# Attention on one core: three weighted bit patterns instead of four in the rows that VectorE exponentiates

## Chip, core and metric

One core of a Trainium2 chip runs the whole program. The metric is the device time of one execution in microseconds. The engines are named as the profile names them: PE (TensorE, matmuls; PEld its weight loads), ACT (ScalarE), DVE (VectorE), POOL (GpSimd, idle after the first microseconds), and SP, which issues most transfers.

## What is computed

```python
B, S, D, H = 1, 2048, 448, 16          # Dh = 28; inputs bf16
qkv = (x @ wqkv).reshape(B, S, 3, H, Dh).transpose(2, 0, 3, 1, 4)
q, k, v = qkv[0], qkv[1], qkv[2]
scores = einsum("bhqd,bhkd->bhqk", q, k) * Dh ** -0.5
p = softmax(scores, axis=-1)
o = einsum("bhqk,bhkd->bhqd", p, v)
return o.transpose(0, 2, 1, 3).reshape(B, S, D) @ wo
```

It is self-attention of 16 heads over 2048 positions with its projections. The kernel takes no maximum out of the scores; at the end it tests the softmax sums, and if they are out of bounds it would run a second, general program (`_general`). On these inputs only the first program (`_fast`) runs.

## The kernel before

**Tiling.** The 16 heads form four groups g of four. A *unit* u is one group and one chunk c of 512 queries: 16 units, u = 4g + c. A unit has 16 key blocks kt of 128 keys. One key block of one unit is a *row*, r = 16u + kt, 256 in all. A row has four *tiles*, one per head: 128 keys by 512 queries of scores, one bank of PSUM.

**Scores (L875).** For each tile PE multiplies KT (28 rows deep, stationary) with QT into a bank. Q is scaled on its way into QT (L512, L514), so that a score is log2 of the wanted exponential, times 1024.

**Exponentials, two ways.** Most rows are *ACT rows*: one activation (L937) takes three banks or two in turn (banks 0 to 2, banks 3 and 4) and writes exponentials in bf16 into PT, a ring of NPT = 47 tile slots; a group of three or two is not split over the end of the ring. 63 rows, listed in `PLAN["rows"]`, are *DVE rows*. For each of their four tiles DVE adds a constant to the score, clamps it at zero and converts it to int16 (L899, tile DY): read as a half float, that bit pattern is a rough exponential. Then it makes, for the whole row at once, copies of the four tiles with 200, 446 and 751 added (L907, tile DS; the numbers are `PHASE`). The errors of the four patterns differ, and their sum is a good exponential. DY and DS have three buffers each. The score banks of DVE rows come from three shared banks ("M"), where the accumulators and the projections live as well.

**Value matmuls (L843, `pv`).** For each row PE multiplies V (stationary, 32 columns a head: 28 of V, a column of ones for the softmax sum, zeros) with the tile's exponentials; four heads run side by side in four column strips, and I call four such matmuls a *pass*. An ACT row takes one pass; a DVE row takes four: one with DY, three with DS, all with the same V, added up in the accumulator. The passes of all rows go in order of the rows.

**Around it.** PE makes xT (L526), the projections to QT and KT (L543) and V (L560), DVE evacuates them (L514, L516), in the first unit as they are needed and later in between. At a unit's end DVE copies the accumulator out (L711), the sums go through DRAM and back (L717 to L725, reciprocal L721), and L727 normalizes into the tile XO; the output projection (L698, L686) follows in the last head group, the last unit has its own tail (L777 to L820). CK and FLAG (L969 to L981) are the test of the sums.

**What sets the order.** Every operation goes to `_Prog.add` with a duration, a priority and what it depends on. `schedule` places all of them on the five engines by these figures, and each engine's instructions are emitted in that order, with semaphores where another engine is waited for. `CFG` and `PLAN` hold the constants: the DVE rows, when late projections are due, how far ahead a DVE row's scores start (`dlead`, in tiles). Where PE would have too little work within a stretch, `fill_to` adds *zero passes* (L472: four matmuls of zeros, added to the open accumulator), and where that can't be done, zero matmuls behind the scores (L878, "padding").

Of the kernel before, what the change touches and what calls it, by code (L numbers as in the profile page):

```python
# [7 lines left out]
ALU = mybir.AluOpType  # L8
AX = mybir.AxisListType
FP32 = mybir.dt.float32  # L10
BF16 = mybir.dt.bfloat16
# [52 lines left out]
class _Prog:  # L64
# [264 lines left out]

LOG2E = 1.4426950408889634  # L330

PHASE = (0, 200, 446, 751)
FONE = 1024.0
ZADD = 15.0 * FONE - FONE * 2.4248887
ZLO = -ZADD


CFG = {"late": 4.5, "load": 1.5, "load0": 18, "dcost": 2.3, "dlead": 31.025180582, "aslack": 232.311784294, "opp": 0.0, "oload": 2.5, "klead": 0.407460656, "vlag": 0.113823454, "hot1": 45000.0, "hotm": 3600.0, "nslack": 2266.270469736, "dlook": 20.0, "plook": 475.482288433, "rcost": 4.9, "rlead": 1.0, "rend": 4, "rgap": 2, "acost": 0.4455, "dprio": -0.035050185, "nride": 2, "rslack": 300.0, "stail": 24, "jprio": -2.321750811, "sdpen": 6.865040263, "rcostx": -0.000676632}

PLAN = {  # L340
    "rows": [9, 14, 19, 20, 25, 33, 36, 39, 43, 48, 51, 52, 54, 61, 62, 69, 75, 79, 80, 85, 87, 95, 96, 98, 103, 108, 110, 115, 117, 120, 131, 133, 134, 140, 142, 144, 148, 149, 154, 160, 170, 172, 176, 177, 178, 180, 184, 191, 194, 197, 201, 207, 211, 212, 215, 218, 223, 225, 229, 231, 239, 240, 241],
    "late": [1.08724689, 1.671681906, 1.586461994, 1.492212309, 1.992884293, 1.888874123, 1.952599148, 2.085365324, 2.327563384, 2.683517599, 2.852937922, 3.53079825, 3.236530611, 3.738744089, 4.578206384, 3.853855012, 4.352187387, 4.127154975, 4.601545874, 4.748366198, 5.016471943, 5.791742663, 6.023704782, 6.452540401, 5.67492232, 6.933850091, 5.567830617, 6.240906859, 8.033147916, 7.787869286, 7.499426139, 7.210279289, 7.346492082, 7.304458952, 7.814524164, 8.966950855, 8.707648667, 8.756221306],
}


def _fast(nc, x, wqkv, wo, out, n_heads=16):
# [9 lines left out]
    NK = NST  # L356
# [2 lines left out]
    NQT = QCH // 128  # L359
    HC = H * 32  # L360
    GD = 4 * DH
    NPT = 47
    NDR = 3
    NDS = 3
    NPH = len(PHASE)
    NMENG = "dve"
# [13 lines left out]
    P = _Prog()  # L380
    es = ExitStack()
    with es:
        def sb(name, shape, dt):
            return es.enter_context(nc.sbuf_tensor(name, shape, dt))
# [7 lines left out]
        QT = sb("QT", [128, G, S], BF16)  # L392
        KT = sb("KT", [128, G, S], BF16)
        V = sb("V", [128, NK, HC], BF16)
        PT = sb("PT", [128, NPT * 512], BF16)
        DY = sb("DY", [128, NDR, 2048], I16)
        DS = sb("DS", [128, NPH - 1, NDS, 2048], I16)
# [12 lines left out]
        ps = es.enter_context(nc.psum_tensor("ps", [128, 8 * 512], FP32))  # L410
# [24 lines left out]
        def load_w(en, t, i0, i1):  # L435
# [11 lines left out]
                      dur=300, prio=-12, name="iota")  # L447
        id_f_op = P.add("dve", lambda e: e.tensor_scalar(id_f[:, :], iota_i[:, :], 0.0, None, ALU.is_equal),
                        deps=[io_op], dur=250, prio=-10, name="id_f")
# [6 lines left out]
        def zero_pass(acc_open, t):  # L456
# [12 lines left out]
            def emit(e):  # L469
                ins = None  # L470
                for h in range(4):
# [13 lines left out]
                       deps=[id_f_op], dur=100, prio=-6, name="sel")  # L485
        grp_wo = _DmaGroup("wo")
        dma_wo = []
        for g in range(G):
            for h in range(4):
# [3 lines left out]
                                    deps=[ms_wop], after=dma_wo[-1:] + [q_last["sp"]], dur=300, prio=-5, name=f"dma_wo{g}{h}", dma_group=grp_wo))  # L493
# [53 lines left out]
            kq_ev[(t, g, c)] = job(f"p{t}_{g}_{c}", prio, mms,  # L547
                                   ((lambda: dst[:, g, c * 512:(c + 1) * 512]), (lambda b: bank(b))), early, evac_eng=eng, mul=QSCALE if t == 0 else None)

        v_ev = {}  # L550

        def proj_v(g, c, prio, early):
            mms = []
# [52 lines left out]
        rows = PLAN["rows"]  # L606
        if rows is None:
# [5 lines left out]
            rows = []  # L613
# [15 lines left out]
        k = 0  # L629
# [194 lines left out]
        def pv(u, kt):  # L824
            g, c = units[u]
            r = u * NK + kt
            if r in n_row:
                ri = n_row[r] % NDR
                rk = n_row[r] % NDS
                terms = [DY[:, ri, :]] + [DS[:, k, rk, :] for k in range(NPH - 1)]  # L830
                parts = [[t_.bitcast(FP16)[:, h * 512:(h + 1) * 512] for h in range(4)] for t_ in terms]
                deps_of = [row_ops[r]] + [[o_] for o_ in row_ev[r]]
                slots = []
            else:
                slots = [tile_slot[(u, kt, h)] for h in range(4)]
                parts = [[PT[:, pi * 512:(pi + 1) * 512] for _, pi in slots]]
                deps_of = [list({id(tile_ev[(u, kt, h)]): tile_ev[(u, kt, h)] for h in range(4)}.values())]

            def f_pv(e, k, p_):
                ins = None  # L840
                b = pv_open[u].banks[0]
                for h in range(4):
                    ins = e.matmul(ps[32 * h:32 * h + 32, b * 512:(b + 1) * 512], V[:, kt, (4 * g + h) * 32:(4 * g + h + 1) * 32],  # L843
                                   p_[h], start=(kt == 0 and k == 0), stop=(kt == NK - 1 and k == len(parts) - 1), tile_position=(0, 32 * h))
                return ins
            base_pr = (u - 60.0 if u == NU - 1 and kt >= NK - 3 else u + (kt + 4) / NK)
            for k, p_ in enumerate(parts):
                first, fin = kt == 0 and k == 0, kt == NK - 1 and k == len(parts) - 1
                op = P.add("pe", (lambda e, k=k, p_=p_: f_pv(e, k, p_)), deps=deps_of[k]
                           + [v_ev[(g, kt // 4)]], acq=(("M", 1) if first else None),  # L850
                           after=[last_pv[0]], kind="c", units=1.0, act=512.0, acc=(True if first else False if fin else None), prio=base_pr, name=f"PV{u}_{kt}" + (f"_{k}" if k else ""))
                last_pv[0] = op
                if first:
                    pv_open[u] = op
                if r in n_row:
                    row_pv[(n_row[r], k)] = op
            for s_ in slots:
                slot_last[s_] = op
            if kt == NK - 1:
                (last_unit if u == NU - 1 else post_unit)(u, op)  # L860
# [7 lines left out]
        n_row = {}  # L868
# [45 lines left out]
        for gi, (kind, idx, b0) in enumerate(items):  # L914
            tl = [tiles[i] for i in idx]
            w = len(tl)
            deps = []
            for (u, kt, h) in tl:
                g, c = units[u]
# [9 lines left out]
            else:  # L929
# [4 lines left out]
                      acq=("M", 1) if b0 is None else None)  # L934
# [3 lines left out]
                       deps=[s] + [slot_last.get(("A", p0 + j)) for j in range(w)], after=[last_exp[0]], dur=66 + w * 426.67, prio=pr, name=f"E{gi}",  # L938
# [10 lines left out]
            if todo_rows and 4 * todo_rows[0] - CFG["dlead"] <= idx[-1] and (nxt < NDS or (nxt - NDS, NPH - 1) in row_pv):  # L949
                r = todo_rows[0]  # L950
# [7 lines left out]
            while pv_next < NT // 4 and all(4 * pv_next + j in done for j in range(4)):  # L958
                u, kt, _ = tiles[4 * pv_next]
# [7 lines left out]
        for lo, hi, rdeps, pr_ in ((0, NE, rs_ops, NU - 0.5), (NE, NE + 16, rs_last, -30.0)):  # L967
# [3 lines left out]
                       deps=[c1], dur=60 + w_, prio=pr_, name=f"CK2_{lo}")  # L971
# [4 lines left out]
        def f_ck(e):  # L976
            b = f_ck.op.banks[0]
            return e.matmul(ps[0:1, b * 512:b * 512 + 1], CKM[:, :], ONE[:, :], start=True, stop=True)
        c4 = P.add("pe", f_ck, deps=[c3, ms_one], dur=100, prio=-34.5, name="CKS", acq=("M", 1))
        f_ck.op = c4  # L980
        P.flag_op = P.add("dve", (lambda e: e.tensor_scalar(FLAG[:, :], ps[0:1, c4.banks[0] * 512:c4.banks[0] * 512 + 1], 127.5, None, ALU.is_ge)),  # L981
                          deps=[c4], dur=80, prio=-34.5, name="FLAG", rel=[(c4, 0)])
# [15 lines left out]
def _general(nc, x, wqkv, wo, out, n_heads=16):  # L998
# [12 lines left out]
    NK = NST  # L1011
# [8 lines left out]
    NPT = 32  # L1020
# [10 lines left out]
    P = _Prog()  # L1031
    es = ExitStack()
    with es:
        def sb(name, shape, dt):
            return es.enter_context(nc.sbuf_tensor("gen_" + name, shape, dt))
# [9 lines left out]
        V = sb("V", [128, NK, HC], BF16)  # L1045
# [14 lines left out]
        ps = es.enter_context(nc.psum_tensor("gen_ps", [128, 8 * 512], FP32))  # L1060
# [10 lines left out]
        for i in range(XG):  # L1071
# [3 lines left out]
                               dur=60, prio=(-10 if i == 0 else -9.7 + 0.01 * i), name=f"dma_x{i}", dma_group=grp, nbytes=(n1 - n0) * 128 * D * 2))  # L1075
        wview = wqkv.rearrange("(it p) c -> p it c", p=IT)
        dma_w = []
        for t in (1, 0, 2):
            grp = _DmaGroup(f"gen_w{t}")
            dma_w.append((t, P.add("sp", (lambda e, t=t: e.dma_start(w_raw[0:IT, :, t * D:(t + 1) * D], wview[:, :, t * D:(t + 1) * D])),  # L1080
                                   dur=60, prio={1: -9.9, 0: -9.8, 2: -9.0}[t], name=f"dma_w{t}", dma_group=grp, nbytes=D * D * 2)))
# [9 lines left out]
        def i32v(ap):  # L1091
# [4 lines left out]
                        deps=[ms_wqk], dur=150, prio=-11, name="ms_wqk1")  # L1096
        ms_wqk2 = P.add("dve", lambda e: e.memset(wqk6[XQ:IT, NIT - 1, 1, :, :, AUGR:AUGR + 3], 0.0),
                        deps=[ms_wqk1], dur=150, prio=-11, name="ms_wqk2")
        io_op = P.add("pool", lambda e: e.iota(iota_i[:, :], [[1, 128]], base=0, channel_multiplier=-1),
                      dur=600, prio=-12, name="iota")  # L1100
# [3 lines left out]
                       deps=[ms_wv], dur=300, prio=-8, name="ms_wv1")  # L1104
        ms_wv2 = P.add("pool", lambda e: e.memset(wv3[XQ:IT, NIT - 1, :, VONE:VONE + 1], 0.0),
                       deps=[ms_wv1], dur=300, prio=-8, name="ms_wv2")
# [5 lines left out]
        for g in range(G):  # L1112
            for h in range(4):
# [3 lines left out]
                                    deps=[ms_wop], after=dma_wo[-1:], dur=60, prio=-5, name=f"dma_wo{g}{h}", dma_group=grp_wo))  # L1117

        id_f_op = P.add("dve", lambda e: e.tensor_scalar(id_f[:, :], iota_i[:, :], 0.0, None, ALU.is_equal),
                        deps=[io_op], dur=250, prio=-10, name="id_f")  # L1120
# [46 lines left out]
        for n0 in range(0, NST, TPB):  # L1167
            for it in range(NIT):
                nn = min(TPB, NST - n0)

                def mk_tr(it=it, n0=n0, nn=nn):
                    def f(e):
                        b = f.op.banks[0]
                        ins = None
                        for j in range(nn):
# [5 lines left out]
                f = mk_tr()  # L1181
                tr = P.add("pe", f, deps=[id_b_op] + xdeps, dur=70 * nn, prio=-10 + 0.001 * n0 + 0.0001 * it, name=f"xT_tr{it}_{n0}",
                           acq=(start_pool(), 1))
                f.op = tr
                en = evac_engine() if n0 < 4 else "act"
                deps = [tr] + ([ms_xT] if it == NIT - 1 else [])
                ev = P.add(en, emit_copy(en, (lambda it=it, n0=n0, nn=nn: xT[0:IT, it, n0 * 128:(n0 + nn) * 128]),
                                         (lambda tr=tr, nn=nn: bank_bf(tr.banks[0])[0:IT, 0:nn * 128])),
                           deps=deps, dur=(nn * 128 + 80) / 1.1, prio=-10 + 0.001 * n0, name=f"xT_ev{it}_{n0}", rel=[(tr, 0)])
# [14 lines left out]

        qt_ev = {}
        kt_ev = {}
        v_ev = {}
        act_only = [False]

        fillers = []  # L1210
# [281 lines left out]
        for j in range(-KOFF, NB + PVLAG + 1):  # L1492
            ja = j + KOFF
            a = a_steps[ja] if 0 <= ja < NA else None
            b = b_steps[j] if 0 <= j < NB else None
            deps = []
# [8 lines left out]
            if b is not None:  # L1505
                ui_b, kt, bp = b
# [9 lines left out]
            if a is not None or b is not None:  # L1516
                qh = []

                def f_qa(e, a=a, b=b, ja=ja, qh=qh):
# [10 lines left out]
                    if b is not None:  # L1530
# [3 lines left out]
                        if a is None:  # L1534
# [3 lines left out]
                           name=f"QA{j}", acq=((("B", 1) if a is not None else ("T", 2)) if b is not None else None))  # L1538
                qh.append(qa)
                last_pe[0] = qa  # L1540
            if a is not None:
# [7 lines left out]
                if (ja % SPU) == 0 and pm_t1[ub] is not None:  # L1549
                    rdeps.append(pm_t1[ub])  # L1550
                red = P.add("dve", (lambda e, o_ap=o_ap, i_ap=i_ap: e.tensor_reduce(o_ap, i_ap, AX.X, ALU.max, negate=True)),
                            deps=rdeps, after=[last_red[0]], dur=1131, prio=float(ui_a), name=f"R{ja}")
# [6 lines left out]
            if b is not None:  # L1559
                ui_b, kt, bp = b  # L1560
                cb, gb = units[ui_b]
                if a is not None:
                    qh2 = []
                    qb = P.add("pe", mk_b(qh2, 2 * bp + 1, gb, kt, cb), deps=[augev_of[ui_b]], after=[last_pe[0]], dur=216, prio=ui_b + 0.5,
                               name=f"QB{j}", acq=("B", 1))
# [5 lines left out]
                for jj, (qop, bi) in enumerate(qops):  # L1571
                    h = 2 * bp + jj
# [20 lines left out]
            while pv_queue and (pv_queue[0][0] <= j or j >= NB):  # L1593
                _, u_, k_, hs_ = pv_queue.pop(0)
# [126 lines left out]
```

## Time and profile before

| | |
|---|---|
| median of three runs | 372.25 us (372.24 to 372.35) |
| the profiled execution | 372.08 us |
| its span | 370.3 us |
| ACT busy | 353.3 us (95%) |
| PE busy | 360.2 us (97%) |
| DVE busy | 336.0 us (91%) |
| POOL busy | 3.4 us |
| transfers | 9.93 MB, 27 GB/s on average |

A busy share is time in which an engine has an instruction under way. PE's matmuls overlap each other and their ends are modelled, so its share says less than the others'; neighbours on ACT and DVE overlap by some hundredths of a microsecond, so an instruction's duration is a little more than its pace. "A <- B" in a row of waits says that A stood until B was done; "issue" is time for which the profile shows no cause. The granted clock is the share of TensorE's clock that the throttle let through.

### The profile page before, as it was taken

To read this page: it belongs to the slowest core of one execution; us is meant where nothing else is said; L and a number is where in the kernel's file an instruction comes from. 1 tells how busy PE (TensorE), PEld (TensorE's weight loads), DVE (VectorE), ACT (ScalarE), POOL (GpSimd) and SP (SyncE) were. 2 spreads that over 40 slices of the span, in tenths; PEclk is the share of its full clock that TensorE was granted. 3 is DMA by queue.
4 is the path that set the end of the run, shared out by engine and by line. 5 is a ranking of instruction groups with operands and counts; after the bars stand their busy time and mean duration, and the time that the engine had idled before them with its cause. 6 is when DMAs were issued, how large, how long until landed. Compare 5 with 4: busy or idle time off the path is not lost.

```text
span 370.3 us, 9208 instructions
## 1 busy us (share of the span) xinstructions
PE 360.2 (97%) x4056; PEld 120.3 (32%) x4056; DVE 336.0 (91%) x581; ACT 353.3 (95%) x314; POOL 3.4 (1%) x9
## 2 busy tenths in 40 slices
PE   8999999999999999999999999999999999999996
PEld 4443233233233233333234322322222222323323
DVE  6578999799999999899999999999999999999613
ACT  2999999999999999999999999999999999999992
POOL 3000000000000000000000000000000000000000
PEclk9999999999999999999999999999999999999999
DMA  8400000000000000000010000000000000100111
GB/s 250 124 2 3 4 29 4 32 2 4 31 2 4 30 18 17 2 12 21 4 32 5 30 3 3 30 4 29 3 31 4 31 2 31 46 10 28 64 40 52
DMA packets 12549, 9.93 MB, mean 27 GB/s; under 512 B 4768, under 2 KB 10656, under 8 KB 12504
## 3 DMA queue, kind: packets, MB, share of 16 engines
q1 hardware_dynamic: 11704, 8.63, 7.7%
q8 instruction: 32, 0.52, 0.6%
q10 hardware_dynamic: 800, 0.66, 0.5%
q14 instruction: 13, 0.11, 0.1%
HBM read 7.23 MB, written 2.06 MB: 25 GB/s over the span
## 4 chain that ended last, share of the span: by engine, by line
ACT 63%; PE 22%; DVE 13%; issue 1%
ACT PT L937 63%; PE ps L875 8%; DVE DY L899 7%; PE ps L843 6%; DVE DS L907 5%; PE ps L543 2%; PE ps L472 2%; PE ps L698 1%; PE ps L560 1%; PE ps L526 1%; DVE OTS L711 0%; PE ps L777 0%; DVE OUTS L686 0%; DVE QT L514 0%; PE ps L746 0%
## 5 line engine op out<-in xcount | busy, mean ns | idle before, releaser
L937 ACT ACTIVATE PT<-ps 128x1536 bf16<-128x1536 f32 (+1 forms) x310 | 350.3, 1379 | 2.9 <-PE ps L875 1.9
L899 DVE TENSOR_SCALAR DY<-ps 128x512 int16<-128x512 f32 x252 | 163.3, 680 | 6.3 <-PE ps L875 5.7
L875 PE MATMUL ps<-QT,KT 28*128 28x512 bf16 x1024 | 162.6, 384 | 4.4 <-ACT PT L937 1.4
L907 DVE TENSOR_SCALAR DS<-DY 128x2048 int16<-128x2048 int16 x189 | 124.8, 679 | 0.3
L875 PEld LDWEIGHTS ps<-QT,KT 28*128 28x128 bf16 x1024 | 42.0, 91 | 132.1 <-ACT PT L937 84.4
L843 PE MATMUL ps<-PT,V 128*32 128x512 bf16 x772 | 66.2, 385 | 0.7 <-DVE DY L899 0.2
L843 PE MATMUL ps<-DS,V 128*32 128x512 f16 x756 | 64.7, 384 | 0.5 <-DVE DS L907 0.2
L543 PE MATMUL ps<-xT,w_raw 112*32 112x512 bf16 x512 | 34.9, 381 | 0.0
L843 PEld LDWEIGHTS ps<-PT,V 128*32 128x32 bf16 x772 | 16.8, 94 | 32.3 <-issue 25.8
L843 PEld LDWEIGHTS ps<-DS,V 128*32 128x32 bf16 x756 | 16.8, 94 | 30.3 <-issue 19.4
L472 PE MATMUL ps<-ZM,ZW 128*32 128x512 bf16 x272 | 25.0, 414 | 1.2 <-DVE ZM L454 1.2
L843 PE MATMUL ps<-DY,V 128*32 128x512 f16 x252 | 24.8, 384 | 0.3 <-DVE QT L514 0.3
L686 DVE CAST OUTS<-ps 128x448 bf16<-128x448 f32 x14 | 8.7, 621 | 9.5 <-PE ps L698 8.6
L560 PE MATMUL ps<-w_raw,xT 112*128 112x112 bf16 x256 | 17.1, 214 | 0.0
L543 PEld LDWEIGHTS ps<-xT,w_raw 112*32 112x32 bf16 x512 | 12.0, 95 | 13.3 <-issue 2.9
L560 PEld LDWEIGHTS ps<-w_raw,xT 112*128 112x128 bf16 x256 | 13.0, 98 | 6.2 <-issue 3.9
L516 DVE CAST KT<-ps 128x512 bf16<-128x512 f32 x16 | 11.0, 685 | 3.6 <-PE ps L543 3.6
L514 DVE TENSOR_SCALAR QT<-ps 128x512 bf16<-128x512 f32 x15 | 10.3, 684 | 1.9 <-PE ps L543 1.9
L698 PE MATMUL ps<-wop,XO 128*128 128x448 bf16 x48 | 11.9, 356 | 0.0
L516 DVE CAST V<-ps 128x448 bf16<-128x448 f32 x16 | 9.9, 616 | 1.3 <-PE ps L560 1.3
L472 PEld LDWEIGHTS ps<-ZM,ZW 128*32 128x32 bf16 x272 | 6.8, 100 | 11.9 <-issue 9.5
L711 DVE COPY OTS<-ps 128x512 f32<-128x512 f32 x15 | 10.2, 679 | 0.0
(50 smaller groups left out, 71.4 us busy)
## 6 DMA issues: line engine op xcount, KB each, us to landing
RB<-scr_r SPq DMA_DIRECT2D x14, 256.0 KB
out_dram<-OUTS SPq DMA_DIRECT2D x14, 112.0 KB, 1.7
XO<-in_x_dram SPq DMA_DIRECT2D x3, 448.0 KB, 7.3
w_raw<-in_wqkv_dram SPq DMA_DIRECT2D x2, 392.0 KB, 6.7
wop<-in_wo_dram SPq DMA_DIRECT2D x16, 24.5 KB
XO<-in_x_dram SPq DMA_DIRECT2D x1, 224.0 KB, 3.5
XO<-in_x_dram ACTq DMA_DIRECT2D x1, 224.0 KB, 3.8
scr_l<-OTS SPq DMA_DIRECT2D x14, 8.0 KB
```

What stands on the lines that cost most here:

```text
L472: ins = e.matmul(ps[32 * h:32 * h + 32, b * 512:(b + 1) * 512], ZW[:, :], ZM[:, :], start=shut, stop=shut, skip_group_check=not shut, tile ...
L514: fe = (lambda e: e.tensor_scalar(evac[0](), evac[1](hold[0].banks[0]), mul, None, ALU.mult))
L516: fe = (lambda e: e.tensor_copy(evac[0](), evac[1](hold[0].banks[0])))
L543: ins = e.matmul(ps[32 * h:32 * h + 32, b * 512:(b + 1) * 512], w_raw[0:IT, it, col:col + 32], xT[0:IT, it, c * 512:(c + 1) * 512], start= ...
L560: ins = e.matmul(ps[:, b * 512 + j * GD:b * 512 + (j + 1) * GD], xT[0:IT, it, n * 128:(n + 1) * 128], w_raw[0:IT, it, 2 * D + g * GD:2 * D ...
L698: return e.matmul(bank(hold[0].banks[0])[:, 0:D], OTN[:, gg, n * 128:(n + 1) * 128], wop[:, gg, :], start=(gg == 0), stop=(gg == G - 1))
L711: accev = P.add("dve", (lambda e: e.tensor_copy(OTS[:, ub, :], bank(pv_open[u].banks[0]))), deps=[last_pv, ots_last[ub]], dur=610, prio=pr ...
L843: ins = e.matmul(ps[32 * h:32 * h + 32, b * 512:(b + 1) * 512], V[:, kt, (4 * g + h) * 32:(4 * g + h + 1) * 32], p_[h], start=(kt == 0 and ...
L875: ins = e.matmul(bank(b), KT[32 * h:32 * h + rows, g, kt * 128:(kt + 1) * 128], QT[32 * h:32 * h + rows, g, c * QCH:(c + 1) * QCH], start= ...
L899: o1 = P.add("dve", (lambda e, ri=ri, h=h, s=s: e.tensor_scalar(DY[:, ri, h * 512:(h + 1) * 512], bank(s.banks[0]), ZLO, ZADD, ALU.max, AL ...
L907: row_ev[r] = [P.add("dve", (lambda e, k=k: e.tensor_scalar(DS[:, k, rk, :], DY[:, ri, :], float(PHASE[k + 1]), None, ALU.add)), deps=row_ ...
L937: ex = P.add("act", (lambda e, p0=p0, w=w, bf=bf: e.activation(PT[:, p0 * 512:(p0 + w) * 512], bank(bf(), w), AF.Exp, scale=ESCALE)), deps ...
```

## The change

A DVE row has three patterns instead of four, with 0, 344 and 682 added, and they are no longer summed alike: their weights are 1, 101/128 and 80/128. The weights are not put on the patterns but on V. A new tile VW holds, for two head groups in turn, two weighted copies of V, which DVE makes from V: for each quarter of the keys (four key blocks, 128x512 elements) of each group in which a DVE row occurs, one scalar multiplication per weight, 32 in all. The first pass of a DVE row reads V as before, the second and third read VW. DS has two parts instead of three, PT has 43 slots instead of 47. There are 67 DVE rows instead of 63, at other places in part, and the constants of the order are new throughout; `vwlead` says how far ahead of its row, in units, a weighted copy is due.

```diff
-PHASE = (0, 200, 446, 751)
+PHASE = (0, 344, 682)
+WTERM = (1.0, 101.0 / 128.0, 80.0 / 128.0)
 FONE = 1024.0
-ZADD = 15.0 * FONE - FONE * 2.4248887
+ZADD = 15.0 * FONE - FONE * 1.6365345
 ZLO = -ZADD
...
-    "rows": [9, 14, 19, 20, 25, 33, 36, 39, 43, 48, 51, 52, 54, 61, 62, 69, 75, 79, 80, 85, 87, 95, 96, 98, 103, 108, 110, 115, 117, 120, 131, 133, 134, 140, 142, 144, 148, 149, 154, 160, 170, 172, 176, 177, 178, 180, 184, 191, 194, 197, 201, 207, 211, 212, 215, 218, 223, 225, 229, 231, 239, 240, 241],
+    "rows": [9, 14, 19, 21, 26, 32, 36, 37, 43, 48, 51, 54, 57, 58, 61, 67, 74, 78, 83, 85, 90, 95, 96, 99, 103, 104, 107, 111, 113, 118, 119, 126, 128, 133, 136, 142, 143, 145, 147, 155, 160, 164, 170, 171, 175, 176, 180, 181, 187, 190, 192, 194, 197, 199, 207, 208, 211, 215, 216, 219, 221, 228, 229, 232, 239, 242, 243],
...
-    NPT = 47
+    NPT = 43
...
+        VW = sb("VW", [128, 2, NPH - 1, NK, 128], BF16)
...
-        v_ev = {}
+        v_ev, vw_ev, vw_used = {}, {}, {}
...
+            if r in n_row and (g, kt // 4) not in vw_ev:
+                c4 = kt // 4
+                vw_ev[(g, c4)] = [P.add("dve", (lambda e, k=k: e.tensor_scalar(VW[:, g % 2, k, 4 * c4:4 * c4 + 4, :], V[:, 4 * c4:4 * c4 + 4, g * 128:(g + 1) * 128],
+                                                                              WTERM[k + 1], None, ALU.mult)),
+                                        deps=[v_ev[(g, c4)], vw_used.get((g % 2, c4))], dur=200, prio=u + kt / NK - CFG["vwlead"], name=f"VW{k}_{g}_{c4}")
+                                  for k in range(NPH - 1)]
+
+            def weights(k, h):
+                return V[:, kt, (4 * g + h) * 32:(4 * g + h + 1) * 32] if k == 0 else VW[:, g % 2, k - 1, kt, 32 * h:32 * h + 32]
...
-                    ins = e.matmul(ps[32 * h:32 * h + 32, b * 512:(b + 1) * 512], V[:, kt, (4 * g + h) * 32:(4 * g + h + 1) * 32],
-                                   p_[h], start=(kt == 0 and k == 0), stop=(kt == NK - 1 and k == len(parts) - 1), tile_position=(0, 32 * h))
+                    ins = e.matmul(ps[32 * h:32 * h + 32, b * 512:(b + 1) * 512], weights(k, h), p_[h], start=(kt == 0 and k == 0), stop=(kt == NK - 1 and k == len(parts) - 1), tile_position=(0, 32 * h))
...
-                           + [v_ev[(g, kt // 4)]], acq=(("M", 1) if first else None),
+                           + [v_ev[(g, kt // 4)] if k == 0 else vw_ev[(g, kt // 4)][k - 1]], acq=(("M", 1) if first else None),
...
+                    if k:
+                        vw_used[(g % 2, kt // 4)] = op
```

In the changed kernel the lines stand a little lower: scores L888, padding L891, exponentials L950, DY L912, DS L920, VW L843, value matmuls L855, zero passes L474.

More of the change, by code (lines that the diff above doesn't have):

```diff
@@ L330 @@
 LOG2E = 1.4426950408889634
-PHASE = (0, 200, 446, 751)
+PHASE = (0, 344, 682)
+WTERM = (1.0, 101.0 / 128.0, 80.0 / 128.0)
 FONE = 1024.0
-ZADD = 15.0 * FONE - FONE * 2.4248887
+ZADD = 15.0 * FONE - FONE * 1.6365345
 ZLO = -ZADD
-CFG = {"late": 4.5, "load": 1.5, "load0": 18, "dcost": 2.3, "dlead": 31.025180582, "aslack": 232.311784294, "opp": 0.0, "oload": 2.5, "klead": 0.407460656, "vlag": 0.113823454, "hot1": 45000.0, "hotm": 3600.0, "nslack": 2266.270469736, "dlook": 20.0, "plook": 475.482288433, "rcost": 4.9, "rlead": 1.0, "rend": 4, "rgap": 2, "acost": 0.4455, "dprio": -0.035050185, "nride": 2, "rslack": 300.0, "stail": 24, "jprio": -2.321750811, "sdpen": 6.865040263, "rcostx": -0.000676632}
+CFG = {"late": 4.5, "load": 1.5, "load0": 18, "dcost": 2.3, "dlead": 31.565328345, "aslack": 232.311784294, "opp": 0.0, "oload": 2.5, "klead": 0.388752986, "vlag": 0.115386484, "hot1": 45000.0, "hotm": 3600.0, "nslack": 2278.659670856, "dlook": 20.0, "plook": 477.119826734, "rcost": 4.9, "rlead": 1.0, "rend": 4, "rgap": 2, "acost": 0.4455, "dprio": 0.137295812, "nride": 2, "rslack": 300.0, "stail": 24, "jprio": -2.367501222, "vwlead": 0.517534586, "sdpen": 6.828329237, "rcostx": -0.000676632}
@@ L340 @@
 PLAN = {
-    "rows": [9, 14, 19, 20, 25, 33, 36, 39, 43, 48, 51, 52, 54, 61, 62, 69, 75, 79, 80, 85, 87, 95, 96, 98, 103, 108, 110, 115, 117, 120, 131, 133, 134, 140, 142, 144, 148, 149, 154, 160, 170, 172, 176, 177, 178, 180, 184, 191, 194, 197, 201, 207, 211, 212, 215, 218, 223, 225, 229, 231, 239, 240, 241],
-    "late": [1.08724689, 1.671681906, 1.586461994, 1.492212309, 1.992884293, 1.888874123, 1.952599148, 2.085365324, 2.327563384, 2.683517599, 2.852937922, 3.53079825, 3.236530611, 3.738744089, 4.578206384, 3.853855012, 4.352187387, 4.127154975, 4.601545874, 4.748366198, 5.016471943, 5.791742663, 6.023704782, 6.452540401, 5.67492232, 6.933850091, 5.567830617, 6.240906859, 8.033147916, 7.787869286, 7.499426139, 7.210279289, 7.346492082, 7.304458952, 7.814524164, 8.966950855, 8.707648667, 8.756221306],
+    "rows": [9, 14, 19, 21, 26, 32, 36, 37, 43, 48, 51, 54, 57, 58, 61, 67, 74, 78, 83, 85, 90, 95, 96, 99, 103, 104, 107, 111, 113, 118, 119, 126, 128, 133, 136, 142, 143, 145, 147, 155, 160, 164, 170, 171, 175, 176, 180, 181, 187, 190, 192, 194, 197, 199, 207, 208, 211, 215, 216, 219, 221, 228, 229, 232, 239, 242, 243],
@@ new lines @@
+    "late": [1.299322759, 1.822557006, 2.163875537, 1.596356936, 2.063296816, 1.856206612, 1.946155059, 2.196917245, 2.351631723, 2.650591028, 2.763613996, 3.528403009, 3.047534614, 3.721148513, 4.223385591, 3.69651624, 3.88002907, 4.051839957, 4.449835317, 4.560752685, 5.643247141, 5.99397256, 6.330386924, 6.513825751, 5.809406098, 6.003720398, 6.187280726, 6.225029866, 8.237463635, 8.012219161, 7.61108487, 7.334748232, 7.574370741, 6.838411391, 7.65064537, 7.734259839, 8.315962664, 7.954788714],
@@ L1206, in _general @@
         kt_ev = {}
-        v_ev = {}
+        v_ev, vw_ev, vw_used = {}, {}, {}
         act_only = [False]
```

## The prediction

> **What bounds the kernel now.** I read the page's busy times first, then the busy time of each engine by stage, then what ACT waited for, and last the chain of waits. The page gives 370.3 us of span and these shares:
>
> ```profile
> PE 360.2 (97%) x4056; PEld 120.3 (32%) x4056; DVE 336.0 (91%) x581; ACT 353.3 (95%) x314; POOL 3.4 (1%) x9
> ```
>
> Three engines are above 90%, so the mean says little. By stage (stage, its length, then busy us of PE, weight loads, DVE, ACT and POOL, then the granted clock):
>
> ```profile
> 10.00:60.00 50.00, 49.10 (x558) 18.01 (x557) 41.68 (x73) 50.00 (x45) 0.00 (x0) 1.00 0.10 26
> 60.00:110.00 50.00, 49.26 (x586) 16.44 (x584) 46.73 (x80) 49.95 (x45) 0.00 (x0) 1.00 0.04 13
> 110.00:160.00 50.00, 49.12 (x576) 17.17 (x576) 48.45 (x83) 49.86 (x45) 0.00 (x0) 1.00 0.05 13
> 160.00:210.00 50.00, 49.74 (x606) 16.54 (x605) 49.14 (x85) 49.57 (x44) 0.00 (x0) 1.00 0.06 19
> 210.00:260.00 50.00, 48.81 (x551) 14.42 (x547) 49.87 (x85) 49.90 (x46) 0.00 (x0) 1.00 0.05 13
> 260.00:310.00 50.00, 48.79 (x532) 13.84 (x531) 49.88 (x87) 50.00 (x46) 0.00 (x0) 1.00 0.04 13
> 310.00:345.00 35.00, 34.55 (x366) 11.39 (x366) 34.93 (x63) 34.12 (x31) 0.00 (x0) 1.00 0.09 30
> ```
>
> ACT has hardly a hole: its largest loss in a 50 us stage is 0.43 us, and 0.88 us from 310 to 345. DVE is as full from 160 to 345 us, but has 8.3 us free from 10 to 60. What ACT waited for (total, times, longest):
>
> ```profile
> ACT QT L512 <- PE ps L543: 5.6, 1, 5.6
> ACT PT L937 <- PE ps L875: 1.9, 3, 0.8
> ACT PT L937 <- PE ps L878: 0.7, 1, 0.7
> ```
>
> The 5.6 us lie before the first exponential; between exponentials ACT waited 1.9 us in three holes. So the span is a head of 10 us, a packed train of exponentials, and a short tail. Pieces of the chain of waits (start, us, what) give the pace of each engine in a row of its own work:
>
> ```profile
> 1.22 3.60 PE ps L472 x32
> 9.99 76.04 ACT PT L937 x67
> 165.12 0.60 DVE DS L907
> 165.72 1.20 DVE DY L899 x2
> 201.63 0.98 PE ps L843 x16
> 310.78 0.76 PE ps L843 x12
> ```
>
> ACT takes 76.04 / 67 = 1.135 us an exponential, 2.27 us for a triple and a pair, 0.454 us a tile. DVE takes 0.60 us for a first step (DY) and 0.60 us for a phase copy (DS), though one lasts 0.68: neighbours overlap. PE takes 0.98 - 0.76 = 0.22 us for four matmuls more.
>
> **The change, ACT.** Four more rows go to DVE, 16 tiles of 772. The order has 151 triples, 151 pairs and one single, where it had 154, 154 and two:
>
> ```profile
> L937 ACT ACTIVATE PT<-ps 128x1536 bf16<-128x1536 f32 x154 | 245.3, 1593 | 2.9 <-PE ps L875 1.9 <-PE ps L878 0.7
> L937 ACT ACTIVATE PT<-ps 128x1024 bf16<-128x1024 f32 x154 | 180.6, 1173 | 0.0
> L937 ACT ACTIVATE PT<-ps 128x512 bf16<-128x512 f32 x2 | 1.2, 718 | 0.0
> ```
>
> That is 3 x 2.27 + 0.6 = 7.4 us off an engine that has no holes, all on the path.
>
> **The change, DVE.** Its groups:
>
> ```profile
> L899 DVE TENSOR_SCALAR DY<-ps 128x512 int16<-128x512 f32 x252 | 163.3, 680 | 6.3 <-PE ps L875 5.7
> L907 DVE TENSOR_SCALAR DS<-DY 128x2048 int16<-128x2048 int16 x189 | 124.8, 679 | 0.3
> L516 DVE COPY xT<-ps 112x512 bf16<-112x512 bf16 x16 | 6.3, 420 | 3.7 <-PE ps L526 3.7
> L969 DVE TENSOR_SCALAR CK<-RS 128x240 f32<-128x240 f32 x1 | 0.3, 275 | 0.0
> ```
>
> 16 first steps more: 16 x 0.60 = +9.6 us. Phase copies 189 to 134: 55 x 0.60 = -33.0 us. New are 32 weighted copies VW of 128x512 bf16, which the trace does not show. From below, a quarter of a phase copy's elements at its pace is 0.15 us; from above, a first step with as many elements is 0.60 us. Below nothing is excluded, as it is added work on a serial engine. I take 0.25 us: the 240-element scalar operation lasts 0.275, the 512-element copy out of PSUM 0.42, and neighbours overlap by 0.08. So +8.0 us (4.8 to 19.2), and DVE falls from 336.0 by 15.4 us (by 4.2 to 18.6). [...]
>
> Where the first copies stand, DVE in the first unit, around the first V cast. Before:
>
> ```order
> L516 COPY xT<-ps 112x512 x4
> L516 CAST V<-ps 128x4x4x28
> L516 CAST KT<-ps 128x512
> L516 COPY xT<-ps 112x512
> L899 TENSOR_SCALAR DY<-ps 128x512
> L516 COPY xT<-ps 112x512 x3
> ```
>
> Now:
>
> ```order
> L518 COPY xT<-ps 112x512 x4
> L518 CAST V<-ps 128x4x4x28
> L843 TENSOR_SCALAR VW<-V 128x512 x2
> L518 CAST KT<-ps 128x512
> L518 COPY xT<-ps 112x512
> L912 TENSOR_SCALAR DY<-ps 128x512
> L518 COPY xT<-ps 112x512 x3
> ```
>
> Two VW have moved in ahead of the KT cast, on which the scores of the third key chunk, and so ACT, wait. The cover is there:
>
> ```profile
> 15.39 0.62 DVE L516 CAST V<-ps 128x448 bf16<-128x448 f32 x1 [1.26 <-PE ps L560]
> 17.00 0.69 DVE L516 CAST KT<-ps 128x512 bf16<-128x512 f32 x1 [0.98 <-PE ps L543]
> ```
>
> DVE stands 0.98 us before that cast; two copies at 0.25 fit, at 0.60 they cost 0.2 us. The other six of this unit lie in the 8.3 us that DVE has free from 10 to 60. Costed at nothing. The new waits: a VW waits for its V cast on the same engine, and for value matmuls two head groups back, long done; a DVE row's second and third passes on PE wait for VW instead of V, with scores for ACT queued behind them. As VW is due half a unit (the constant 0.52) ahead of its row, the row's own phase copy stays the later of the two, and this wait is costed at nothing too.
>
> From 160 us on DVE has no such holes, so the balance counts there. From row 96 to the last DVE row the plan before has 41 DVE rows and 105 ACT rows; the new one 45 and 103. ACT needs 4 x 0.454 = 1.815 us a row: 190.6 and 186.9 us. DVE needs 41 x 7 x 0.60 = 172.2 us, now 45 x 6 x 0.60 = 162.0. For its other work it had 18.4 us, and has 24.9, out of which ten VW take 2.5. So it is looser than before by some 4 us, and by 0.5 us even with VW at 0.60. The pattern in the last DVE rows, DVE before:
>
> ```order
> L899 TENSOR_SCALAR DY<-ps 128x512 x2
> L721 RECIPROCAL RS<-LT 128x16
> L907 TENSOR_SCALAR DS<-DY 128x2048 x2
> L899 TENSOR_SCALAR DY<-ps 128x512 x2
> L907 TENSOR_SCALAR DS<-DY 128x2048
> L899 TENSOR_SCALAR DY<-ps 128x512 x2
> L907 TENSOR_SCALAR DS<-DY 128x2048
> ```
>
> Now:
>
> ```order
> L912 TENSOR_SCALAR DY<-ps 128x512 x4
> L920 TENSOR_SCALAR DS<-DY 128x2048
> L912 TENSOR_SCALAR DY<-ps 128x512 x2
> L920 TENSOR_SCALAR DS<-DY 128x2048
> L912 TENSOR_SCALAR DY<-ps 128x512 x2
> L729 TENSOR_TENSOR XO<-RB,OTS 128x512
> L912 TENSOR_SCALAR DY<-ps 128x512 x2
> ```
>
> Fewer copies stand between first steps, so score banks come free sooner.
>
> **The change, PE.** Its groups:
>
> ```profile
> L843 PE MATMUL ps<-PT,V 128*32 128x512 bf16 x772 | 66.2, 385 | 0.7 <-DVE DY L899 0.2
> L843 PE MATMUL ps<-DS,V 128*32 128x512 f16 x756 | 64.7, 384 | 0.5 <-DVE DS L907 0.2
> L472 PE MATMUL ps<-ZM,ZW 128*32 128x512 bf16 x272 | 25.0, 414 | 1.2 <-DVE ZM L454 1.2
> L843 PE MATMUL ps<-DY,V 128*32 128x512 f16 x252 | 24.8, 384 | 0.3 <-DVE QT L514 0.3
> L878 PE MATMUL ps<-ZM 28*128 28x512 bf16 x3 | 0.4, 374 | 0.0
> ```
>
> A DVE row takes three passes of four matmuls instead of four: 1780 value matmuls become 1560, 55 passes less, 55 x 0.22 = -12.1 us. The order has 316 zero matmuls for 272 (+11 passes, +2.4 us) and 17 padding matmuls in the scores for 3 (at most +3.1 us). PE's work falls by about 7 us. ACT waits for PE in three holes only, so this gains nothing by itself; up to the 1.9 us of holes could go, and I count none. Stationary operands from VW instead of V load the same 128x32.
>
> **The sum.** The profiled execution took 372.08 us, its span 370.3. 372.08 - 7.4 = 364.7 us. The median of the three runs lies 0.17 above the profiled one, so I forecast 364.8 us, with 363.3 to 366.3 as this case's own range (holes gone or doubled).
>
> **The rivals.** *The ring.* PT shrinks from 47 tile slots to 43. In groups of 3 and 2 that are not split over the end, 45 of the 47 were in use, and 42 or 43 will be. The tightest place before (PE matmuls and ACT exponentials on PT up to 233.70 and 234.20 us, then the pass):
>
> ```profile
> 0.00:233.70 233.70, 39.33 (x448) 9.89 (x448) 222.99 (x197) 1.00 0.09 27
> 0.00:234.20 234.20, 39.77 (x457) 10.12 (x460) 223.49 (x197) 1.00 0.09 27
> 233.76 0.83 PE L843 MATMUL ps<-PT,V 128*32 128x512 bf16 x12
> ```
>
> 98 triples and 98 pairs and one triple make 493 tiles written; the next pair, at 234.3, overwrites tiles 449 and 450, whose matmuls began at 233.76. That is almost no room, and with two or three slots fewer ACT would stand there for 0.9 to 1.4 us. It is this wait that would take the place of the holes. Against it: the delay came from value matmuls queued behind phase copies, and of those a third goes. At one such place 366.0 us, at three 368.5.
>
> *The change is slower.* The scheduler's zero passes are there for the clock, and PE now has 7 us less to do. With cold PE, at the start, eight passes took 3.60 us, 0.45 a pass against 0.22. If PE fell to that pace in thinned stretches, each us of full work would take two: 15 us of such stretches lose about 7.4 us and eat the gain, which is the point from which it decides; 20 us lose 10, 364.8 + 10 = 374.8 us. For it: the added padding shows stretches in which too little was left to do. Against it: no stage of the table above has PE under 97% busy, and the plan adds zero passes where work goes. [...]
>
> *DVE takes over.* If VW cost 0.60 us and bunched where V casts stand, DVE would be behind by 10 x 0.35 = 3.5 us after 160 us, of which the 4 us of new room cover most; what is left locally I put at 2 us: 366.8 us.
>
> **How the numbers follow.** Forecast 0.70; ring 0.10; DVE 0.07; cold PE 0.09; the holes gone and a better packed tail (below 363.3) 0.04. The first two rivals that give back time stay below 368.5, so a range of 363.0 to 368.5 leaves out the cold PE and a sliver below, under 2 in 10. 0.2% of 372 us is 0.7 us, about what a measurement of this kernel tells from no change. All cases but the cold PE are faster by more: 0.89 faster; slower 0.09, and 0.02 for a give-back that just cancels.
>
> **What would show it.** Right: ACT busy near 345.9 us (353.3 - 7.4) with under 3 us of idle before L950; DVE near 320 us; VW at 0.2 to 0.35 us each; head and tail as before. Wrong: ACT waiting for PE's value matmuls or standing before triples (ring); zero or value matmuls of 0.6 us after the start (cold); DVE full and ACT with holes at the VW copies (DVE). Were ACT idle up by over 3 us, the step that takes the 7.4 us as wholly on the path would be wrong.

## The result, and the profile after

The changed kernel takes 364.02 us (median, 363.72 to 364.31), against 372.25 us: a ratio of 0.978, 95% interval 0.976 to 0.980. A second set of runs gave 363.77 us and 0.977 (0.976 to 0.979). The profiled execution took 364.01 us with a span of 362.2 us. The page's busy times, after:

```profile
PE 350.9 (97%) x3894; PEld 118.1 (33%) x3894; DVE 321.4 (89%) x574; ACT 345.9 (95%) x307; POOL 3.4 (1%) x9
```

ACT is busy 7.4 us less, the 7.4 of the sum. By stage, after, with the same columns as in the prediction (five of the seven stages):

```profile
10.00:60.00 50.00, 48.61 (x575) 18.80 (x567) 39.85 (x76) 49.72 (x45) 0.00 (x0) 1.00 0.11 28
160.00:210.00 50.00, 49.45 (x548) 15.46 (x540) 49.27 (x87) 49.96 (x45) 0.00 (x0) 1.00 0.05 15
210.00:260.00 50.00, 48.45 (x550) 15.99 (x547) 47.67 (x85) 49.95 (x45) 0.00 (x0) 1.00 0.04 13
260.00:310.00 50.00, 49.35 (x530) 14.09 (x529) 49.94 (x87) 50.00 (x46) 0.00 (x0) 1.00 0.06 18
310.00:345.00 35.00, 34.35 (x333) 11.75 (x331) 30.39 (x54) 34.04 (x31) 0.00 (x0) 1.00 0.11 37
```

ACT is as packed as before, DVE still full from 160 to 210 and from 260 to 310, and 4.5 us emptier in the stage from 310 to 345. What ACT waited for, after:

```profile
ACT QT L514 <- PE ps L545: 5.9, 1, 5.9
ACT PT L950 <- PE ps L888: 1.1, 3, 0.7
ACT PT L950 <- PE ps L891: 0.7, 1, 0.7
```

These rows leave out the shortest waits. All idle time of ACT in front of its exponentials stands in the page's row of that group, before and after (the figure behind the second bar):

```profile
L937 ACT ACTIVATE PT<-ps 128x1536 bf16<-128x1536 f32 (+1 forms) x310 | 350.3, 1379 | 2.9 <-PE ps L875 1.9
L950 ACT ACTIVATE PT<-ps 128x1536 bf16<-128x1536 f32 (+1 forms) x303 | 342.9, 1356 | 1.9 <-PE ps L888 1.1
```

Neighbours on ACT overlap by more than the hundredths of a microsecond given for them ahead, by about 0.22 us: in the changed kernel an exponential lasts 1.356 us in the mean, and one takes 342.9 / 303 = 1.13 us of busy time. The holes went from 2.9 to 1.9 us, and the head grew by 0.3 us in this execution. So -7.4 (work) - 1.0 (holes) + 0.3 (head) = -8.1 us, which is what the span is shorter by. The groups that the prediction priced:

```profile
L950 ACT ACTIVATE PT<-ps 128x1536 bf16<-128x1536 f32 x151 | 236.7, 1568 | 1.0 <-PE ps L891 0.7 <-PE ps L888 0.2
L912 DVE TENSOR_SCALAR DY<-ps 128x512 int16<-128x512 f32 x268 | 174.6, 682 | 10.7 <-PE ps L888 10.0
L920 DVE TENSOR_SCALAR DS<-DY 128x2048 int16<-128x2048 int16 x134 | 90.0, 680 | 0.6
L843 DVE TENSOR_SCALAR VW<-V 128x512 bf16<-128x512 bf16 x32 | 8.1, 283 | 0.1
L474 PE MATMUL ps<-ZM,ZW 128*32 128x512 bf16 x316 | 28.6, 410 | 1.2 <-DVE ZM L456 1.2
```

DVE now waits 10.0 us for scores, where it waited 5.7 before: it has become the engine that waits. A weighted copy lasts 0.283 us, and all 32 together take 8.1 us.

### The profile page after: what moved, and what is told of

Its sections match the earlier page's. It is cut to its first block, busy times and chain, and to the rows that moved or that the text cites. A ratio compares the mean times of both kernels' runs of the same rounds, so it can differ in the third digit from the quotient of the medians.

```text
span 362.2 us, 8855 instructions
## 1 busy us (share of the span) xinstructions
PE 350.9 (97%) x3894; PEld 118.1 (33%) x3894; DVE 321.4 (89%) x574; ACT 345.9 (95%) x307; POOL 3.4 (1%) x9
## 4 chain that ended last, share of the span: by engine, by line
ACT 73%; PE 23%; DVE 3%; issue 0%
ACT PT L950 73%; PE ps L888 8%; PE ps L855 7%; PE ps L474 2%; PE ps L700 2%; PE ps L545 2%; DVE DY L912 2%; PE ps L562 1%; PE ps L528 1%; PE ps L779 1%; DVE DS L920 0%; PE ps L759 0%; PE ps L822 0%; PE ps L798 0%; PE ps L748 0%
## 5 line engine op out<-in xcount | busy, mean ns | idle before, releaser
L950 ACT ACTIVATE PT<-ps 128x1536 bf16<-128x1536 f32 (+1 forms) x303 | 342.9, 1356 | 1.9 <-PE ps L888 1.1
L912 DVE TENSOR_SCALAR DY<-ps 128x512 int16<-128x512 f32 x268 | 174.6, 682 | 10.7 <-PE ps L888 10.0
L888 PE MATMUL ps<-QT,KT 28*128 28x512 bf16 x1024 | 164.1, 383 | 6.2 <-ACT PT L950 2.7
L920 DVE TENSOR_SCALAR DS<-DY 128x2048 int16<-128x2048 int16 x134 | 90.0, 680 | 0.6
L888 PEld LDWEIGHTS ps<-QT,KT 28*128 28x128 bf16 x1024 | 42.2, 91 | 127.4 <-ACT PT L950 84.4
L855 PE MATMUL ps<-PT,V 128*32 128x512 bf16 x756 | 66.0, 386 | 0.5 <-DVE OTS L713 0.2
L855 PE MATMUL ps<-DS,VW 128*32 128x512 f16 x536 | 47.4, 384 | 0.2 <-DVE DS L920 0.2
L545 PE MATMUL ps<-xT,w_raw 112*32 112x512 bf16 x512 | 36.1, 382 | 0.0
L474 PE MATMUL ps<-ZM,ZW 128*32 128x512 bf16 x316 | 28.6, 410 | 1.2 <-DVE ZM L456 1.2
L855 PEld LDWEIGHTS ps<-PT,V 128*32 128x32 bf16 x756 | 16.7, 94 | 34.7 <-issue 28.7
L855 PE MATMUL ps<-DY,V 128*32 128x512 f16 x268 | 26.4, 385 | 0.2
L855 PEld LDWEIGHTS ps<-DS,VW 128*32 128x32 bf16 x536 | 12.7, 94 | 18.3 <-issue 12.8
L474 PEld LDWEIGHTS ps<-ZM,ZW 128*32 128x32 bf16 x316 | 7.7, 99 | 15.2 <-issue 11.4
L855 PEld LDWEIGHTS ps<-DY,V 128*32 128x32 bf16 x268 | 7.0, 94 | 11.4 <-issue 7.7
```

Source lines behind the costliest of these rows:

```text
L888: ins = e.matmul(bank(b), KT[32 * h:32 * h + rows, g, kt * 128:(kt + 1) * 128], QT[32 * h:32 * h + rows, g, c * QCH:(c + 1) * QCH], start= ...
L912: o1 = P.add("dve", (lambda e, ri=ri, h=h, s=s: e.tensor_scalar(DY[:, ri, h * 512:(h + 1) * 512], bank(s.banks[0]), ZLO, ZADD, ALU.max, AL ...
L920: row_ev[r] = [P.add("dve", (lambda e, k=k: e.tensor_scalar(DS[:, k, rk, :], DY[:, ri, :], float(PHASE[k + 1]), None, ALU.add)), deps=row_ ...
L950: ex = P.add("act", (lambda e, p0=p0, w=w, bf=bf: e.activation(PT[:, p0 * 512:(p0 + w) * 512], bank(bf(), w), AF.Exp, scale=ESCALE)), deps ...
```

## The experiments

**One half of the change at a time.** First the weights alone: the three weighted patterns, the copies and the ring of 43, on the plan of before.

```diff
-PHASE = (0, 200, 446, 751); four passes with V; NPT = 47
+PHASE = (0, 344, 682); WTERM, VW and weights(k, h) as in the change; NPT = 43
 PLAN and CFG as before, 63 rows
```

> Three weighted patterns with the weighted copies of V and the ring of 43, but the 63 DVE rows, the due times and the order constants of the kernel before. ACT keeps its 772 tiles; DVE loses 63 phase copies and gains 32 weighted copies (-37.8 + 8.1 = -29.7 us, to about 306 us busy); PE loses 63 passes (-13.9 us) and gets zero passes in their place. Theory (the time is the number of tiles on ACT, and ACT has only 1.9 us of holes to lose): 370.3 to 372.5 us. Rival (the gain came from the lighter DVE and PE): 366 us or less, most of the 8 us.

Measured: 373.26 us, ratio 1.002 (1.000 to 1.004). Page and ACT's waits:

```profile
PE 358.9 (97%) x4070; PEld 119.3 (32%) x4070; DVE 311.3 (84%) x550; ACT 353.8 (95%) x314; POOL 3.4 (1%) x9
ACT PT L950 <- PE ps L888: 2.4, 5, 1.5
```

DVE is 24.7 us lighter and nothing is gained; ACT has its 353.8 us of work. The time is 0.8 us above the theory's range: the order that results has longer waits for scores than the one before (2.4 us, one of them 1.5, against 1.9), not shorter ones. The rival, that lighter DVE and PE bring the gain, falls. An order fitted to these rows was not tried, but it could win little more than those 2.4 us: the rest of the train is ACT's own work.

Then the rows alone: four plain patterns and V as before, on the plan of the changed kernel.

```diff
 PHASE = (0, 200, 446, 751); four passes with V; NPT = 47
-63 rows, due times and CFG of before
+67 rows, due times and CFG of the changed kernel
```

> Four plain patterns and the ring of 47 as before, but the 67 DVE rows, due times and order constants of the changed kernel. ACT has 756 tiles (345.9 us busy); DVE has 4 x 7 x 0.60 = 16.8 us more than before (about 353 us). Theory (moving tiles pays only where DVE has room, and the third phase copy was that room): from row 96 on DVE needs 45 x 7 x 0.60 = 189 us and some 18 us of other work, where ACT needs 187 us; ACT gets some 15 to 20 us of holes, 376 to 386 us. Rival (the tiles moved bring the gain whatever a DVE row costs): 364 to 366 us.

Measured: 399.59 us (394.43 to 402.43), ratio 1.067 (1.059 to 1.074).

```profile
PE 382.0 (96%) x4268; PEld 127.0 (32%) x4268; DVE 354.1 (89%) x609; ACT 347.9 (87%) x307; POOL 3.4 (1%) x9
ACT PT L937 <- PE ps L843: 22.9, 10, 5.4
ACT PT L937 <- PE ps L875: 7.6, 8, 1.9
210.00:260.00 50.00, 47.25 (x461) 12.22 (x453) 41.84 (x71) 36.25 (x32) 0.00 (x0) 0.83 0.04 13
246.07 0.10 PEld L843 LDWEIGHTS ps<-DS,V 128*32 128x32 bf16 x4 [0.23 <-DVE DS L907]
246.74 1.45 ACT L937 ACTIVATE PT<-ps 128x1536 bf16<-128x1536 f32 x1 [3.84 <-PE ps L843]
```

The direction is the theory's, the size is not: 27 us instead of 4 to 14. ACT has 16 tiles less to do, and stands for 30 us waiting for scores and value matmuls. Most of that is the ring: its slots come free late, because the value matmuls of L843 come late. In front of the hole of 3.84 us they stand behind a pass that waits for its phase copy; the longest hole, 5.4 us, lies in the tail, where PE does output projections between them, so phase copies aren't the whole of it. In the stage from 210 to 260 us the granted clock fell to 0.83 on average, which would be 17 us of 50 at half clock and which the expectation had not counted. As those constants were laid for the changed mix, part of the 27 us may be the order's; this run doesn't separate that. Neither half gains anything alone.

**The retuning.** The changed kernel with the old constants and due times:

```diff
 67 rows, weights, VW, NPT = 43
-CFG and "late" of the changed kernel
+CFG and "late" of the kernel before (with vwlead)
```

> The changed kernel with its 67 rows, weights and ring, but the order constants and the due times of the late projections of the kernel before. ACT keeps 756 tiles (345.9 us busy), DVE its 321 us. Theory (with three engines nearly full the order has to be laid anew for the new mix, or ACT gets holes): ACT's busy time unchanged and 3 to 6 us more of waits for PE, 366.5 to 370 us. Rival (the constants are small corrections): 363.5 to 364.6 us.

Measured: 371.29 us (369.11 to 372.04), ratio 0.995 (0.992 to 0.998).

```profile
ACT PT L950 <- PE ps L888: 7.6, 9, 2.7
210.00:260.00 50.00, 46.26 (x477) 12.49 (x477) 44.27 (x74) 45.21 (x41) 0.00 (x0) 0.93 0.06 19
```

The rows are the same, ACT's work nearly so (347.1 us busy), and 7 of the 8 us are gone into 7.6 us of waits for scores, most of them in this one stage. One run kept a granted clock of 1.00 and took 369.11 us; the others had 0.991 to 0.995. So 5 us are the order, and up to 3 us more come with a clock that relapsed, as it did in none of the nine executions of the changed kernel. The new constants are not decoration: with the old ones, the whole change brings 1 us (371.29 against 372.32 us for the kernel before on the same chip).

**Is DVE off the path?** The changed kernel with its order kept, and a second, unused copy behind each weighted copy:

```diff
+for each VW in the finished order of DVE:
+    behind it: VX = V * weight            # same size, read by nobody
-NPT = 43
+NPT = 39                                 # room for VX
```

> The changed kernel in its own order, instruction by instruction, with a second, unused copy behind each of the 32 weighted copies (into a tile of its own; the ring is 39 slots to make room for it, of which at most 35 were in use). DVE gets 8.1 us more work, 2.5 to 3 us of it after 160 us, where DVE is full. Theory (DVE has come off the path: ACT's lead over it holds some microseconds): 364.0 to 365.5 us. Rival (DVE is the bound, or close to it): its 8.1 us show for the most part, 369 to 372 us.

Measured: 364.75 us (364.63 to 364.79), ratio 0.979 (0.977 to 0.981).

```profile
PE 351.0 (97%) x3894; PEld 117.5 (32%) x3894; DVE 326.8 (90%) x606; ACT 346.5 (95%) x307; POOL 3.4 (1%) x9
ACT PT L951 <- PE ps L889: 1.3, 4, 0.7
```

DVE's busy time rose by 5.4 us and not by the 8.1 expected (5.4 / 32 = 0.17 us for each, where one lasts 0.292: neighbouring copies overlap more than I took), and the time by 0.7 us. So over the whole run DVE has some microseconds to give. The run says little of the two stages in which DVE is full: only four of the 32 copies fell into the one from 160 to 210 us, and none into the one from 260 to 310 us. That DVE doesn't hold ACT up there rests on the stage rows of the changed kernel, which have ACT busy 49.96 and 50.00 of 50 us. With 39 slots ACT never waited for value matmuls either.

**The ring.** The kernel before with 43 slots, first with the order that the scheduler makes for that, then with the order of 47 kept:

```diff
-NPT = 47
+NPT = 43
```

> The kernel before with 43 tile slots instead of 47 and nothing else (the scheduler lays the order anew for it). Theory (the ring bound the kernel before at its tightest place, where 45 tiles were in flight): ACT stands there for 0.9 to 1.4 us, with longer waits for PE before its pairs, 373.0 to 373.8 us. Rival (a ring of 43 is free, before as after): 371.9 to 372.5 us.

```diff
 order and priorities as with NPT = 47
+slots and the waits for their readers from a ring of 43
```

> The kernel before in its own order, instruction by instruction, but with tiles laid into a ring of 43 slots instead of 47, and each exponential waiting for the matmuls that last read its slots. Theory (the ring rival of the prediction: one tight place, two or three tiles short): 0.9 to 1.4 us more, 373.0 to 373.7 us, ACT waiting for L843 near 234 us; then the rest of the 4.9 us of the ring of 43 with a new order came from that order. Rival (the ring itself costs it): 376 to 378 us.

Measured: with a new order 377.01 us, ratio 1.013 (1.012 to 1.015), outside what either theory gave. With the order kept 374.49 us (373.35 to 378.46), ratio 1.007 (1.004 to 1.010); its five runs at a granted clock of 0.999 or 1.00 lie at 373.35 to 373.71, the six at 0.982 to 0.995 above that. ACT's waits and the place, with the order kept:

```profile
ACT PT L945 <- PE ps L843: 1.1, 2, 0.9
234.10 0.83 PE L843 MATMUL ps<-PT,V 128*32 128x512 bf16 x12
234.55 2.36 ACT L945 ACTIVATE PT<-ps 128x1536 bf16<-128x1536 f32 x2 [0.94 <-PE ps L843]
```

That is the rival's mechanism at the place and of the size that the prediction gave it: 0.94 us at 234.55 us, and 1.3 us in time at full clock. The other 3.4 us of the ring of 43 came from the new order. What relieves the ring is the lighter DVE row: with 43 slots, the same 63 rows and the old constants, ACT waited 1.4 us for value matmuls with four patterns (first of the two runs above) and not at all with three (weights alone). In the changed kernel the ring is not short. At its fullest (PE and ACT instructions on PT until then):

```profile
0.00:346.98 346.98, 62.39 (x708) 15.72 (x708) 335.47 (x296) 1.00 0.09 26
```

296 exponentials are 740 tiles, 708 of them read; with the triple that starts next, 35 are in flight, 8 under the 43.

**The clock.** The changed kernel without zero passes after the start, and then, with its order kept, with only every second one:

```diff
-if level >= self.FILL_TARGET or (...)
+if t > self.HOT_UNTIL or level >= self.FILL_TARGET or (...)
```

> The changed kernel without zero passes and padding after the first 10 us (32 and 3 zero matmuls stay of 316 and 17). Theory A (PE's clock needs them): matmuls of about 0.6 us appear after the start, PE falls behind by 0.5 us for each us of full work at half pace, and the time rises by over 3 us. Theory B (PE's real work is dense enough): no such matmuls, PE's work is off the path, 363.3 to 364.7 us.

```diff
+drop every second zero pass after 10 us from the finished order of PE
```

> The changed kernel in its own order with every second zero pass after the first 10 us left out (about 35 of 71); the padding stays. Theory (the zero passes hold the clock with little to spare): stretches of granted clock 0.5 appear, and each us of them costs about 0.32 us as without any zero passes (52.5 us for 164 us of half clock); 368 to 385 us. Rival (half of them are enough): granted clock 1.00 throughout and 363.5 to 364.5 us.

Measured: 406.68 us (400.54 to 417.53) without, ratio 1.081 (1.076 to 1.087); 378.83 us (374.06 to 382.69) with half of them, ratio 1.009 (1.006 to 1.013). Both spread with the share of half clock that an execution catches. Stages without any after the start, then with half of them (the row from 134 to 152 us lies within one relapse: its granted clock is 0.50):

```profile
110.00:160.00 50.00, 48.62 (x446) 13.53 (x448) 41.22 (x71) 43.30 (x38) 0.00 (x0) 0.75 0.04 13
310.00:345.00 35.00, 34.45 (x251) 7.12 (x252) 28.07 (x48) 28.67 (x25) 0.00 (x0) 0.60 0.05 15
ACT PT L950 <- PE ps L888: 43.5, 46, 2.0
```

```profile
110.00:160.00 50.00, 48.96 (x471) 14.24 (x470) 41.50 (x72) 43.94 (x40) 0.00 (x0) 0.80 0.05 13
260.00:310.00 50.00, 47.63 (x465) 12.53 (x453) 47.39 (x81) 48.48 (x44) 0.00 (x0) 0.93 0.05 13
134.00:152.00 18.00, 18.00 (x132) 4.56 (x127) 12.31 (x21) 12.26 (x11) 0.00 (x0) 0.50 0.05 16
PE ps L888 <- ACT PT L950: 4.4, 16, 0.6
ACT PT L950 <- PE ps L888: 15.9, 20, 1.7
```

In the profiled executions the mean clock was 0.802 over 414.7 us and 0.928 over 380.6 us, which is 2 x 0.198 x 414.7 = 164 us and 2 x 0.072 x 380.6 = 55 us of half clock, if every relapse is at the 0.50 of that row; the spans are 52.5 and 18.4 us longer than the changed kernel's, 0.32 and 0.34 us for each of them. The fastest executions of the two, at 0.854 and 0.959, give 0.31 and 0.33 in the same way. So the 284 zero matmuls after the start, with the padding, are work of no value that carries the result, and half of the zero passes are too few.

**A version beyond both.** Where the runs pointed, ring to spare and some DVE room, I spent four slots of the ring on a fourth DY buffer and moved one more row, with the order laid anew:

```diff
-NPT = 43; NDR = 3; 67 rows
+NPT = 39; NDR = 4; 68 rows, due times and CFG laid anew
```

> A version built on what the runs showed: the changed kernel with four slots of the ring given up (43 to 39; at most 35 were in use) for a fourth DY buffer, 68 DVE rows instead of 67, and the rows, due times and constants laid anew for that. ACT has 752 tiles: one row less is 1.8 us less; DVE has 3.6 us more, of which the doubled copies showed that about 5 us more cost 0.7 us. Theory (ACT sets the time as long as the order keeps it fed): 362.0 to 363.3 us. Rival (the last room is used up, or the clock relapses somewhere): 364 us or more, with holes before ACT or a granted clock under 1.00.

> The changed kernel as it is, on the same chip as the run with four buffers, to compare the two: 363.7 to 364.3 us, granted clock 1.00.

Measured on the same chip: 363.89 us (363.29 to 364.03), ratio 0.978 (0.976 to 0.979), beside 363.77 us (363.54 to 364.05), ratio 0.977 (0.976 to 0.979), for the changed kernel as it is. No gain. The four-buffer version:

```profile
PE 350.1 (97%) x3902; PEld 116.3 (32%) x3902; DVE 324.3 (90%) x580; ACT 344.1 (95%) x306; POOL 3.4 (1%) x9
ACT PT L950 <- PE ps L888: 1.8, 5, 0.7
ACT PT L950 <- PE ps L855: 0.9, 1, 0.9
```

ACT's work is the expected 1.8 us less, and 1.6 us came back as holes, 0.9 of it waiting for value matmuls, so at the ring of 39. Whether the four slots would have spared it no run shows; the changed kernel's own order did without them when its copies were doubled. The rival holds, and no version here beats the changed kernel.

## Why the prediction was right, point by point

- **The sum.** 364.8 us was forecast, 364.02 us measured. The term on ACT, 7.4 us, is the measured 353.3 - 345.9. That it lay wholly on the path is shown by the span, which is made up of ACT's work, its holes, the head and an unchanged tail of 7.8 us (-7.4 - 1.0 + 0.3 = -8.1 us), and from two sides by runs: with the tiles back on ACT (weights alone) the gain is gone, with 5.4 us more of DVE work it stays.
- **The holes.** I counted none of the holes as gone; of 2.9 us 1.0 went, and the head took 0.3 back. That is most of the 0.8 us by which the forecast was high. Why those holes closed no run takes apart; the head differs between executions of one program (ACT's first wait was 5.9 us in this profile of the changed kernel, 5.7 us in that of the second set).
- **The weighted copies.** 0.25 us of pace was taken; 8.1 / 32 = 0.253 was measured, and 0.283 us for one alone.
- **DVE and PE.** DVE was to fall by 15.4 us to near 320 and fell to 321.4; PE by about 7 and fell by 9.3, nearly all of it without effect by itself, as weights alone shows.
- **The ring.** Mechanism, place and size were right where it applies, in the kernel before; that a third of the phase copies gone relieves it was right too. That 42 or 43 of the 43 slots would be in use was not: at most 35 were.
- **The slower rival.** The clock was a real danger, held off by the order's zero passes (406.68 us without them and the padding after the start, 378.83 us with half of them). The prediction's price of 0.5 us for each us of half clock was too high: 0.32 to 0.34 without zero passes or with half of them. With all of them it was somewhat more: the profiled run with the old constants had 2 x 0.009 x 370.1 = 6.7 us of half clock and a span 2.8 us longer than the run at 1.00 (367.3 us), 0.42. By these the point of decision lies at some 18 to 23 us of half clock, not 15. The granted clock doesn't show the slow pace of the first passes: they take 0.45 us each against 0.22, and the first 3 us of the kernel before have 1.00 in that column. Later it shows a relapse plainly, as in the row with 0.50. With half of the zero passes the low clock came back in a stage in which PE was busy 48.96 of 50 us, and after the start PE never waited longer than 0.6 us at a time.
- **What the prediction passed over.** It found room on DVE and PE in the order that the changed kernel came with, and costed the new waits at nothing. That held for this order. But the order is worth 7 of the 8 us (5 where the clock stays at 1.00): with the old constants the same sum would have been 6.5 us too low (371.29 us), and the prediction has no term that would tell a fitted order from another.

## What to carry to other kernels

Where one engine is packed and two more are nearly full, price a change by the work that it takes off the packed engine, and ask of the others only whether they have room. Expect that room alone gives nothing (weights alone, 24.7 us less of DVE at a ratio of 1.002), and that work moved without room can cost several times what it was to gain (rows alone, 27 us against 7.4). An order fitted to one mix has to be fitted again for another before the change is judged: here the same change was worth 1 us with the old order and 8 us with its own. Judge the clock by its own column, not by how busy PE is (0.80 with PE busy 48.96 of 50 us).

## What had not been expected of the hardware

A TensorE that the profile has almost wholly busy can drop to half clock: with every second zero pass gone, the stage from 110 to 160 us shows PE busy 48.96 of 50 us at a granted clock of 0.80, and from 134 to 152 us busy all the time at 0.50. The loss per microsecond of half clock was 0.32 to 0.34 us there. And in some kernels (the old constants on the new rows, the ring of 43 with its order kept) some executions kept a clock of 1.00 and others of the same program did not, with up to 3 and 5 us between them. The kernel before isn't free of it: 8 of its 39 executions beside the experiments had a granted clock of 0.995 or less and took 373.6 us or more, while all nine of the changed kernel had 0.999 or 1.00; nine are too few to call that a property of its order.
